# A fused attention and mixer kernel: the transposed copy of u made by VectorE and DMA instead of TensorE, and the second pass reordered

## The chip, the cores and the metric

The kernel runs on one core of one Trainium2 chip. The metric is the device time of one launch in microseconds (us). Before the change it is 831.86 us, the median of three runs from 831.58 to 831.9.

A core has five engines that run side by side, each with its own queue that it works through in order: TensorE (PE; its weight loads are listed as PEld), VectorE (DVE), ScalarE (ACT), GpSimd (POOL) and SyncE (SP). They wait for each other by semaphores. SP and ScalarE also issue DMAs, which sixteen DMA engines carry out.

## What is computed

```python
kv  = einsum('bhsd,bhse->bhde', k, v)            # 8 batches, 8 heads, 576 rows, 64 per head
out = einsum('bhsd,bhde->bhse', q, kv)
x   = out / sqrt(mean(out*out, -1) + 1e-6) * g   # then laid out as (8, 576, 512)
h   = maximum(x.T @ w_tok1, 0) @ w_tok2          # over the 576 rows, 256 in between
u   = x + h.T
out = u + maximum(u @ w_ch1, 0) @ w_ch2          # 512 -> 1536 -> 512
```

All is float32. The change concerns the last line, the "second pass" over u.

## The kernel before

**First pass.** Attention and token mixing run over pairs of batches and store u to DRAM (`u_dram`). Nine groups of 512 rows come of it: eight batches' first 512 rows, and one of the 64 remaining rows of each.

**Second pass.** For each group two products follow: u with w_ch1 (with relu), and the result v with w_ch2. Each is made by Strassen's scheme at two levels, so 7 x 7 = 49 block products in place of 64. A block product is three matmuls of 128 x 128 x 128. The blocks that go into them are sums of blocks: of u (`outer_u`, `inner_u`), of the weights (kept in DRAM as `sums_dram` and loaded 576 KB at a time into one of three `sums` tiles by `fetch_sums`), and of v (`split`, `inner`, the halves A, S1 to S4). Group 0 goes through `channel1_once` and `channel2_once` with one level only, while the weights' sums are made. Groups 1 to 8 go through `channel1(g, n0)` and `channel2(g, n0)`.

**Order.** The order of groups 1 to 8 is written by hand. A product has a place; the seven inner products of one outer product stand at the places of `PLACE`, and the next outer product begins seven places later, so that two are interleaved. `put(place, step)` sets steps of other engines behind a product. 49 places are a first product, the next 49 a second one, 98 a group. `keep` holds each engine to the order in which its instructions are written.

**Banks.** `outer` uses three PSUM banks. Bank a collects products 1, 6, 7 and 4, and is read after each of them (`read`: a copy on ScalarE, or an add on VectorE where `base` gives something to add). Bank c holds product 2, bank b products 5 and 3. `write` adds what was read to bank b or c, on VectorE. So product 6 must wait for the read after product 1, 7 for that after 6, 4 for that after 7, and product 3 for the `write` that reads bank b after product 5. Each has about two products' time for it.

**The transposed u.** The products need u with its columns on the partitions. `fetch_t` loads a tile of 128 rows x 512 from `u_dram` (`xt`, two buffers); `turn_u` transposes its four 128 x 128 blocks on TensorE into PSUM (`ps_ut`, line 515) and copies them to `uT` on ScalarE. For group g + 1 this happens in the second product of group g, at places 11, 15, 19 and 23 of it. There is one `uT`: it can be overwritten when the first product of group g is over. Its sums are made by VectorE at the end of the second product and at the start of the next group.

**Queues.** All of the second pass's DMAs are issued by SP: loads of the weights' sums (14 a group), of tiles of u (`xt` four, `xg` two, for the final sum) and stores of the result (two). Results of the second product are gathered in `r` tiles and added by VectorE (`radd`, `xadd`) to `xg`.

Of the kernel before, what the change touches and what calls it, by code (L numbers as in the profile page):

```python
# [19 lines left out]
def kernel(  # L20
# [85 lines left out]
    def do(f, *a):  # L106
        return lambda: f(*a)
# [394 lines left out]
    def fetch_t(g, i):  # L502

        if g < NG:
            xt[g, i] = late["xt"].tile([P, DM], F32, name="xt")
            dma(xt[g, i], u_dram[g][ts(i, P)])

    def turn_u(g, i, psum):
        if g >= NG:
            return  # L510
        if i == 0:
            uT[g] = late["u"].tile([P, 7, 7, P], F32, name="uT")
        pt = psum()
        for c in range(NC):
            keep(nc.tensor.transpose(pt[:, c], xt[g, i][:, ts(c, P)], ident))  # L515
        o, n = 2 * (i // 2), 2 * (i % 2)
        copy(uT[g][:, o:o + 2, n:n + 2], pt.rearrange("p (o n) t -> p o n t", o=2))

    def outer_u(g):

        return t_sums(lambda n: uT[g][:, SB[n], :4]) if g < NG else []

    def inner_u(g, lo, hi):

        return t_sums(lambda n: uT[g][:, lo:hi, SB[n]]) if g < NG else []

    V = {}

    def m_psum(shape, name):
        return late["m"].tile(shape, F32, name=name, tag="m")  # L530

    def t_psum():
        return late["t"].tile([P, NC, P], F32, name="ps_ut")

# [19 lines left out]
    def channel1_once(g):  # L554
# [4 lines left out]
        def pair(d):  # L559
# [3 lines left out]
            def product(n, ps, start, stop):  # L563
                for w in range(2):
                    i, f = divmod(2 * d + w, W)
                    for c in range(2):
                        wt = w_ch1[:, SA[n]] if SA[n] < 4 else late["w2"][:, SA[n] - 4]
                        matmul(ps[:, w], lhsT=wt[:, 2 * i + c, ts(f, P)],
                               rhs=uT[g][:, SB[n], c:4:2],
                               start=(start and w == 0 and c == 0), stop=stop,  # L570
                               skip_group_check=True)
# [104 lines left out]
    def outer(place, size, mul, to, base=None):  # L676
# [11 lines left out]
        def temp(n, bufs):  # L688
            t[n] = late["tmp"].tile([P, FQ], F32, name=n, tag=n, bufs=bufs)[:, :size]
            return t[n]  # L690

        def fit(flat, like):
            return flat if len(like.shape) == 2 else flat.rearrange("p (w t) -> p w t", w=W)

        def read(o, i, j):

            a = fit(banks["a"], to(i, j))
            o = fit(o, to(i, j)) if len(o.shape) == 2 else o
            if base:
                tensor_add(o, a, base(i, j))  # L700
            else:
                copy(o, a)

        def write(i, j, name, n):
            o = to(i, j)
            tensor_add(o, fit(banks[name], o), fit(t[n], o))

# [28 lines left out]

    ORDER1, ORDER2 = (1, 6, 2, 7, 5, 3, 4), (1, 4, 6, 5, 7, 2, 3)
    order = [(w, g, o) for g in range(1, NG) for w, os in ((1, ORDER1), (2, ORDER2)) for o in os]
    sums, v_in_parts = {}, {}

    def fetch_sums(n):
        if n < len(order):
            w, _, o = order[n]
            sums[n] = sums_tile()
            dma(sums[n], sums_dram[w, o])

# [5 lines left out]
    def channel1(g, n0):  # L752
# [4 lines left out]
        def first(i, o):  # L757
            n = n0 + i

            def mul(p, ps, start, stop):  # L760
                for w in range(W):
                    matmul(ps[:, ts(w, P)], lhsT=part(1, o, p, sums[n])[:, ts(w, P)],
                           rhs=uT[g][:, SB[o], SB[p]], start=(start and w == 0), stop=stop,
                           skip_group_check=True)

            base = {2: 1, 5: 3, 4: 1}.get(o)
            outer(7 * n, FQ, mul, lambda i, j: sub(v_tile(g, TO[o]), i, j),
                  base and (lambda i, j: sub(v_tile(g, base), i, j)))
            put(7 * n + PLACE[3] + 1, do(fetch_sums, n + 3))
# [15 lines left out]
        for t, *places in ((2, 25, 29, 28, 25), (7, 47, 47, 48, 48), (1, 53, 57, 53, 54)):  # L785
            for place, (i, j) in zip(places, ((0, 0), (0, 1), (1, 0), (1, 1))):
                rectify(place, t, i, j)
        if g > 1:
            steps = outer_u(g)[1:]
            for place, step in zip((0, 0, 2, 3, 4, 5, 7, 9), steps + [inner_u(g, 1, 2)[2]] + inner_u(g, 2, 7)):  # L790
                put(b + place, step)

    def channel2(g, n0):
# [3 lines left out]
        def second(i, o):  # L797
# [14 lines left out]

            outer(7 * n, P, mul, to)
            put(7 * n + PLACE[3] + 1, do(fetch_sums, n + 3))
            return r

        rs = {o: second(i, o) for i, o in enumerate(ORDER2)}

        def inner(o):
# [23 lines left out]

            return begin, steps[1], own if o == 1 else steps[2], steps[3]

# [28 lines left out]
        for place, steps in (  # L874
                (-17, [ins[1][0], ins[1][2]]), (-16, [ins[1][1]]), (-14, [ins[1][3]]),
                (1, [A[0], ins[4][0]]), (2, [A[1]]), (4, [ins[4][1], S1[0]]), (6, [ins[4][3], S1[1]]),
                (7, [ins[4][2]]), (8, [S2[0]]), (9, [S2[1]]), (11, [ins[6][0]]), (12, [S4[0]]),
                (13, [ins[6][1], S4[1]]), (15, [ins[6][3], ins[6][2]]), (17, [ins[5][0], S3[0]]),
                (19, [ins[5][1], S3[1]]), (20, [xadd(0, 0, 1)]), (21, [ins[5][3], ins[5][2]]),
                (23, [ins[7][0], xadd(1, 0, 4)]), (25, [ins[7][1]]), (26, [ins[7][2], ins[7][3]]),  # L880
                (28, [ins[2][0]]), (29, [radd(6, 1)]), (30, [ins[2][1], xadd(0, 1, 6)]),
                (32, [ins[2][3], ins[2][2]]), (34, [ins[3][0]]), (36, [xadd(0, 1, 5), ins[3][1]]),
                (37, [xadd(1, 1, 5)]), (38, [ins[3][3], ins[3][2]]), (43, [radd(7, 6)]),
                (44, [xadd(1, 0, 7)]), (45, [xadd(1, 1, 7)])):
            put(b + place, *steps)

        if g < NG - 1:
            for place, steps in ((57, [do(store, g, xg, 1)]), (59, [xadd(0, 0, 2)]), (63, [xadd(0, 1, 3)]),
                                 (71, [do(store, g, xg, 0)]), (78, [do(fetch_x, g + 1, 0)]),
                                 (85, [do(fetch_x, g + 1, 1)])):  # L890
                put(b + place, *steps)
        else:
# [4 lines left out]

            put(b + 49, xadd(0, 0, 2), do(store, g, xg, 1))
            put(b + 50, do(last, 0, 0))
# [3 lines left out]

        for i in range(J):
            place = b + 12 + 4 * i
            put(place - 12, do(fetch_t, g + 1, i)) if i < 2 else None
            put(place - 1, do(turn_u, g + 1, i, t_psum))
            put(place, do(fetch_t, g + 1, i + 2)) if i < 2 else None

        if g + 1 < NG:  # L910
            first, second, _, fourth = inner_u(g + 1, 0, 2)
            put(b + 40, first)
            put(b + 41, second)
            put(b + 42, fourth)
            put(b + 46, outer_u(g + 1)[0])
# [127 lines left out]
    late["xg"] = pool("xg", 1)  # L1043
    late["xt"] = pool("xt", 2)
    late["u"] = pool("u", 1)
    fetch_t(0, 0)
    fetch_t(0, 1)
    fill = [list(rounding), mix_ch1()]
    woven = fill[0][:4] + fill[1] + fill[0][4:]

    def turn(g, i, psum):
        turn_u(g, i, psum)
        if i + 2 < J:
            fetch_t(g, i + 2)

    u_psum = lambda: ps["o"].tile([P, NC, P], F32, name="ps_ut", tag="o")
    last = [
        "h00 2 -s40 2", "h01 2", "h10 2", "h11 2", "hr 1", "c0 u0 1", "c1 u1 1", "c2 u2", "c3 u3 1", "u4",
        "c4 u5 1", "u6 1", "u7", "u8"]
    more = {f"c{i}": do(turn, 0, i, u_psum) for i in range(J)}  # L1060
    more[f"c{J}"] = lambda: [f() for f in outer_u(0)]
# [3 lines left out]
    psums.close()  # L1065
    right.close()
    late["v"] = pool("v", 1, "right")
    late["r"] = pool("r", 4, "right")
# [4 lines left out]
    late["d2"] = pool("d2", 1, "right").tile([P, 3, NS, DH], F32, name="d2")  # L1073
    late["m"] = pool("m", 6, space=bass.MemoryType.PSUM)
    late["t"] = pool("t", 2, space=bass.MemoryType.PSUM)


    fetch_x(0, 0)
    fetch_x(0, 1)
    fetch_t(1, 0)  # L1080
    fetch_t(1, 1)
    firsts, lasts = mix_ch2()
    inner1 = [split(1, o) for o in ORDER1]
    inner2 = [split(2, o) for o in ORDER2]
    weave(channel1_once(0), firsts + [f for fs, _ in inner1 for f in fs])
    for n in range(3):
        fetch_sums(n)
    extra = [do(turn, 1, i, t_psum) for i in range(J)]
    extra += [lambda: [f() for f in outer_u(1)], lambda: [f() for f in inner_u(1, 0, 7)], lambda: None]
    body = [step for pair in zip(channel2_once(0), extra) for step in pair]  # L1090
    weave(body, lasts + [f for fs, _ in inner2 for f in fs] + [f for _, f in inner1])
# [49 lines left out]
```

## Time and profile before

| what | value |
|---|---|
| median of three runs | 831.86 us |
| the profiled execution | 832.03 us |
| its span, first to last instruction | 830.2 us |
| TensorE's transposes of u | 144, in 36 tiles, 188.8 to 738.9 us |
| ScalarE's copies of them | 36, 586 ns each |
| loads of sums, SP, 576 KB | 112, 3.8 us to landing |
| loads of u tiles, SP, 256 KB | 36, 3.5 us to landing |
| VectorE add, 128 / 384 / 512 / 768 elements | 283 / 548 / 680 / 948 ns |
| granted clock of TensorE | 0.999 |

The span is cut by stage: attention and token mixing to 206 us; group 0's first product to 243 and its second to 281; then eight groups of about 68 us to 826. Slices of the second pass look alike, so one group can be read for all:

```profile
416.60:484.90 68.30, 68.25 (x611) 68.02 (x610) 58.94 (x120) 22.78 (x61) 7.29 (x4) 1.00 0.53 172
484.90:553.20 68.30, 68.25 (x611) 68.02 (x610) 58.94 (x120) 22.90 (x61) 7.30 (x4) 1.00 0.53 169
```

The columns are the stretch in us, its length, busy time (and instructions) of PE, PEld, DVE, ACT and POOL, the granted clock, the share of the DMA engines and GB/s. A full engine is no proof that it sets the pace at every place: one also has to see in which half of a group each is full, and what waits for what there.

### The profile page before, as it was taken

The numbers are of one execution on the slowest core, as the hardware profiler recorded it, in microseconds if no ns is written. First come the engines' busy times: TensorE is split into PE (matmuls) and PEld (weight loads), VectorE is DVE, ScalarE is ACT, GpSimd is POOL, SyncE is SP. The second block draws the span as 40 slices with busy tenths as digits, with TensorE's granted clock in tenths as the row PEclk, the third lists the DMA queues.
The fourth block names the chain that finished last, engine by engine and source line by source line (L and its number), as shares of the span: only waits on it lengthen the run. The fifth ranks groups of instructions, "written<-read, shape, count | busy, mean of one in ns | idle before, by whom it ended". The sixth has DMA issues, their size and how long they took to land.

```text
span 830.2 us, 16562 instructions
## 1 busy us (share of the span) xinstructions
PE 812.6 (98%) x6528; PEld 719.9 (87%) x6528; DVE 701.8 (85%) x1334; ACT 289.1 (35%) x777; POOL 76.9 (9%) x59
## 2 busy tenths in 40 slices
PE   6999999999999999999999999999999999999997
PEld 6655555644888899999999999999999999999997
DVE  4688989999785979978977987997897897798696
ACT  1346665562210124234234323322423322333321
POOL 1200101010000020003003003001100300300300
PEclk9999999999999999999999999999999999999999
DMA  9999996422436445365356446546536545644642
GB/s 296 325 341 319 337 364 244 153 89 102 174 127 220 175 169 170 118 194 200 128 165 216 144 141 204 181 140 193 192 115 191 185 149 145 216 164 141 190 144 80
DMA packets 67966, 156.57 MB, mean 189 GB/s; under 512 B 5296, under 2 KB 24752, under 8 KB 67888
## 3 DMA queue, kind: packets, MB, share of 16 engines
q1 hardware_dynamic: 66208, 153.77, 56.6%
q10 hardware_dynamic: 1680, 1.74, 0.7%
q8 instruction: 52, 0.85, 0.4%
q14 instruction: 26, 0.21, 0.1%
HBM read 128.35 MB, written 27.13 MB: 187 GB/s over the span
## 4 chain that ended last, share of the span: by engine, by line
PE 88%; DVE 9%; issue 1%; DMA 1%; ACT 1%; SPq 0%; ACTq 0%; DVEq 0%
PE ps_a L127 35%; PE ps_b L127 18%; PE ps_c L127 9%; PE ps_h L127 6%; PE ps_u L127 6%; PE ps_v L127 4%; PE ps_w L127 3%; PE ps_o L127 3%; PE ps_ut L515 2%; PE ps_kv L127 2%; DVE sv L118 1%; DMA raw<-in_moe_w_tok_dram 1%; DVE v L118 1%; DVE x L379 1%; DVE ms L399 1%
## 5 line engine op out<-in xcount | busy, mean ns | idle before, releaser
L124 ACT COPY u<-ps_a 128x128 f32<-128x128 f32 (+1 forms) x176 | 60.5, 344 | 176.5 <-PE ps_a L127 164.6
L118 POOL TENSOR_TENSOR v<-v,v 128x768 f32<-128x768 f32 x32 | 58.4, 1856 | 553.0 <-ACT t L124 553.0
L127 PE MATMUL ps_b<-uT,sums 128*128 128x128 f32 x672 | 85.5, 275 | 0.0
L127 PEld LDWEIGHTS ps_b<-uT,sums 128*128 128x128 f32 x672 | 80.2, 192 | 0.0
L127 PE MATMUL ps_a<-uT,w_ch 128*128 128x128 f32 x576 | 78.8, 275 | 0.0
L127 PEld LDWEIGHTS ps_a<-uT,w_ch 128*128 128x128 f32 x576 | 71.5, 192 | 0.1
L118 DVE TENSOR_TENSOR v<-ps_b,u 128x384 f32<-128x384 f32 x112 | 60.2, 550 | 12.9 <-PE ps_b L127 12.9
L127 PE MATMUL ps_u<-h,w_tok 128*128 128x512 f32 (+1 forms) x160 | 67.0, 601 | 0.0
L127 PE MATMUL ps_h<-x,w_tok 128*128 128x512 f32 (+1 forms) x160 | 65.8, 603 | 0.8 <-ACT x L424 0.8
L118 DVE TENSOR_TENSOR v<-v,v 128x768 f32<-128x768 f32 (+1 forms) x70 | 64.1, 926 | 0.3
L118 DVE TENSOR_TENSOR uT<-uT 128x512 f32<-128x512 f32 (+4 forms) x103 | 63.1, 628 | 1.1
L124 ACT COPY t<-ps_a 128x128 f32<-128x128 f32 (+1 forms) x88 | 30.3, 344 | 92.7 <-PE ps_a L127 85.3
L121 ACT ACTIVATE v<-v 128x384 f32<-128x384 f32 (+1 forms) x102 | 49.3, 526 | 30.7 <-DVE v L118 26.6
L127 PE MATMUL ps_a<-uT,w 128*128 128x128 f32 x432 | 58.7, 275 | 0.0
L118 DVE TENSOR_TENSOR u<-ps_a,v 128x384 f32<-128x384 f32 x48 | 26.8, 558 | 32.1 <-PE ps_a L127 31.6
L127 PEld LDWEIGHTS ps_h<-x,w_tok 128*128 128x128 f32 (+1 forms) x160 | 25.9, 189 | 31.9 <-issue 28.1
L127 PEld LDWEIGHTS ps_a<-uT,w 128*128 128x128 f32 x432 | 53.4, 192 | 0.0
L118 DVE TENSOR_TENSOR xg<-xg,r 128x512 f32<-128x512 f32 (+1 forms) x78 | 50.7, 661 | 0.8 <-ACT r L124 0.6
L424 ACT ACTIVATE x<-x,inv 128x64 f32<-128x64 f32 x184 | 46.0, 335 | 9.5 <-DVE inv L419 8.1
L127 PE MATMUL ps_a<-uT,sums 128*128 128x128 f32 x336 | 46.9, 276 | 1.3 <-ACT t L124 1.3
L127 PE MATMUL ps_a<-sums,sv 128*128 128x128 f32 x336 | 47.3, 277 | 0.9 <-ACT r L124 0.5
L127 PEld LDWEIGHTS ps_u<-h,w_tok 128*128 128x128 f32 (+1 forms) x160 | 24.5, 179 | 27.1 <-issue 22.4
(123 smaller groups left out, 1650.1 us busy)
## 6 DMA issues: line engine op xcount, KB each, us to landing
sums<-sums SPq DMA_DIRECT2D x112, 576.0 KB, 3.8
qT<-in_q_dram SPq DMA_DIRECT2D x8, 1152.0 KB, 9.5
xt<-u_dram SPq DMA_DIRECT2D x36, 256.0 KB, 3.5
xg<-u_dram SPq DMA_DIRECT2D x18, 512.0 KB, 4.9
k_in<-in_k_dram SPq DMA_DIRECT2D x16, 512.0 KB, 9.2
u_dram<-x SPq DMA_DIRECT2D x16, 512.0 KB, 3.6
out_dram<-xg SPq DMA_DIRECT2D x16, 512.0 KB, 5.4
sums<-sv SPq DMA_DIRECT2D x14, 576.0 KB, 2.8
```

The costliest lines, as they stand in the source:

```text
L118: keep(engine.tensor_tensor(out=o, in0=a, in1=b, op=op))
L121: keep(nc.scalar.activation(o, a, AF.Relu))
L124: keep(nc.scalar.copy(o, a))
L127: keep(nc.tensor.matmul(*a, **kw))
L379: keep(nc.vector.tensor_mul(heads(X[pair, c][:, t]), heads(bank[c, t]), g_sb.to_broadcast([P, H, D])))
L399: keep(nc.vector.tensor_reduce(stats_of(c)[0][:, ts(t, H)], sq[c, t], axis=AX.X, op=ALU.add))
L424: keep(nc.scalar.activation(x[:, i], x[:, i], AF.Copy, scale=inv[:, i]))
L515: keep(nc.tensor.transpose(pt[:, c], xt[g, i][:, ts(c, P)], ident))
```

## The change

It has four parts, all in the second pass.

1. `turn_u` gives way to `turn_blocks` and `fetch_u`. VectorE transposes each 32 x 32 block of a tile within its 32 partitions (two instructions of 128 x 256 a tile) into `y`. After two tiles, four DMAs write `y` to DRAM (`blocks_dram`), and later four DMAs read it back so that the blocks come to lie as in the full transpose. `uT` gets the shape [128, 7, 4, 7, 32], so the sums and TensorE's moving operand read rows of 32. In groups 1 to 8 there is one buffer of `xt` and one of `y`; the turning stands in the first product (places 2 to 34), the reading back at places 8 and 10 of the second.
2. Sums are loaded on ScalarE's queue.
3. The outer products of the second product run in the order 1, 4, 2, 6, 5, 7, 3 in place of 1, 4, 6, 5, 7, 2, 3; product 6's read adds result 1 at once (so four VectorE reads in place of four ScalarE copies and one `radd`), and the steps beside the products get new places, some behind the product.
4. The two PSUM banks of the transposes go to the products (eight in place of six).

```diff
-            xt[g, i] = late["xt"].tile([P, DM], F32, name="xt")
+            xt[g, i] = late["xt" if g else "xt0"].tile([P, DM], F32, name="xt")
...
-        pt = psum()
-        for c in range(NC):
-            keep(nc.tensor.transpose(pt[:, c], xt[g, i][:, ts(c, P)], ident))
-        o, n = 2 * (i // 2), 2 * (i % 2)
-        copy(uT[g][:, o:o + 2, n:n + 2], pt.rearrange("p (o n) t -> p o n t", o=2))
+    def turn_blocks(g, i):
+        if g >= NG:
+            return
+        half, n = i // 2, 2 * (i % 2)
+        if n == 0:
+            xt[g] = late["y" if g else "y0"].tile([P, NC, 2, NC, Q], F32, name="y")
+        for o in range(2):
+            keep(nc.vector.transpose(
+                xt[g][:, :, o, n:n + 2].rearrange("p b n t -> p n b t"),
+                xt[g, i][:, ts(o, DH)].rearrange("p (n b t) -> p n b t", n=2, b=NC)))
+        if n:
+            t = blocks_dram[g, half] = dram.tile([Q, NC, 2, NC, P], F32, name=f"blocks{g}{half}")
+            for a in range(NC):
+                dma(t[:, :, :, a], xt[g][ds(a * Q, Q)].rearrange("p b o n t -> p b o (n t)"))
+
+    def fetch_u(g, half):
+        if g >= NG:
+            return
+        if half == 0:
+            uT[g] = late["u"].tile([P, 7, NC, 7, Q], F32, name="uT")
+        for b in range(NC):
+            dma(uT[g][ds(b * Q, Q), 2 * half:2 * half + 2, :, :4].rearrange("p o a n t -> p o a (n t)"),
+                blocks_dram[g, half][:, b])
...
-        return t_sums(lambda n: uT[g][:, lo:hi, SB[n]]) if g < NG else []
+        return t_sums(lambda n: uT[g][:, lo:hi, :, SB[n]]) if g < NG else []
...
-    ORDER1, ORDER2 = (1, 6, 2, 7, 5, 3, 4), (1, 4, 6, 5, 7, 2, 3)
+    ORDER1, ORDER2 = (1, 6, 2, 7, 5, 3, 4), (1, 4, 2, 6, 5, 7, 3)
...
-            dma(sums[n], sums_dram[w, o])
+            dma(sums[n], sums_dram[w, o], nc.scalar)
...
-                           rhs=uT[g][:, SB[o], SB[p]], start=(start and w == 0), stop=stop,
+                           rhs=uT[g][:, SB[o], :, SB[p]], start=(start and w == 0), stop=stop,
...
+        for place, f, i in ((2, fetch_t, 0), (16, turn_blocks, 0), (18, fetch_t, 1), (22, turn_blocks, 1),
+                            (24, fetch_t, 2), (28, turn_blocks, 2), (30, fetch_t, 3), (34, turn_blocks, 3)):
+            put(b + place, do(f, g + 1, i))
...
-            outer(7 * n, P, mul, to)
+            outer(7 * n, P, mul, to, o == 6 and (lambda i, j: rs[1][0][:, i, ts(j, P)]))
...
-            for place, steps in ((57, [do(store, g, xg, 1)]), (59, [xadd(0, 0, 2)]), (63, [xadd(0, 1, 3)]),
-                                 (71, [do(store, g, xg, 0)]), (78, [do(fetch_x, g + 1, 0)]),
+            for place, steps in ((58, [radd(7, 6)]), (60, [xadd(1, 1, 5)]), (61, [xadd(1, 0, 7)]),
+                                 (62, [xadd(1, 1, 7)]), (63, [do(store, g, xg, 1)]), (65, [xadd(0, 1, 5)]),
+                                 (66, [xadd(0, 1, 3)]), (71, [do(store, g, xg, 0)]), (78, [do(fetch_x, g + 1, 0)]),
...
-        for i in range(J):
-            place = b + 12 + 4 * i
-            put(place - 12, do(fetch_t, g + 1, i)) if i < 2 else None
-            put(place - 1, do(turn_u, g + 1, i, t_psum))
-            put(place, do(fetch_t, g + 1, i + 2)) if i < 2 else None
+        put(b + 8, do(fetch_u, g + 1, 0))
+        put(b + 10, do(fetch_u, g + 1, 1))
...
-    late["xt"] = pool("xt", 2)
+    late["xt"] = pool("xt", 1)
...
-    late["m"] = pool("m", 6, space=bass.MemoryType.PSUM)
-    late["t"] = pool("t", 2, space=bass.MemoryType.PSUM)
+    late["y"] = pool("y", 1, "right")
+    late["m"] = pool("m", 8, space=bass.MemoryType.PSUM)
```

For groups 0 and 1 the turning is woven into the end of the first pass and into group 0's first product, with two buffers each for group 0.

## The prediction

> **What bounds the kernel now.** I read the page's busy totals and chain of waits first, then the timeline of TensorE over one group of the second pass, then VectorE's over the same group, and last the stretches of that group in a table of windows.
>
> ```profile
> PE 812.6 (98%) x6528; PEld 719.9 (87%) x6528; DVE 701.8 (85%) x1334; ACT 289.1 (35%) x777; POOL 76.9 (9%) x59
> ...
> PE 88%; DVE 9%; issue 1%; DMA 1%; ACT 1%; SPq 0%; ACTq 0%; DVEq 0%
> ```
>
> TensorE is never without work; 88% of the chain that ends last is TensorE. In the second pass (from 280.7 us) the timeline of TensorE shows, in start, duration and group:
>
> ```profile
> 349.06 0.83 PE L127 MATMUL ps_a<-uT,w_ch 128*128 128x128 f32 x6
> 349.73 0.83 PE L127 MATMUL ps_c<-uT,w_ch 128*128 128x128 f32 x6
> ...
> 389.93 0.60 PE L515 MATMUL ps_ut<-ident,xt 128*128 128x128 f32 x4
> 390.36 0.93 PE L127 MATMUL ps_b<-w_ch,sv 128*128 128x128 f32 x6
> ...
> 416.85 0.83 PE L127 MATMUL ps_a<-uT,w_ch 128*128 128x128 f32 x6
> ```
>
> A block product (three matmuls) starts 0.67 us after the one before; four transposes of u take 0.43. A group, from one first product to the next, takes 416.85 - 349.06 = 67.79: 98 products are 65.66, sixteen transposes 1.74, and 0.4 is waits. The windows of this group (length, then PE, PEld, DVE, ACT, POOL busy, clock, DMA share, GB/s) are its first product, most of its second, and the rest:
>
> ```profile
> 349.06:382.56 33.50, 33.50 (x303) 33.50 (x302) 24.79 (x47) 11.64 (x26) 7.29 (x4) 1.00 0.57 176
> 382.56:411.08 28.52, 28.47 (x255) 28.23 (x254) 28.48 (x60) 9.99 (x30) 0.00 (x0) 1.00 0.49 165
> 411.08:416.85 5.77, 5.77 (x55) 5.77 (x53) 5.15 (x14) 1.07 (x4) 0.00 (x0) 1.00 0.46 157
> ```
>
> The second line is the one to see: during the second product VectorE is busy 28.48 of 28.52 us. Two engines are full there, and the transposes that TensorE does in that stretch are also time in which VectorE catches up. In the first product VectorE has 8.7 us to spare, ScalarE much everywhere.
>
> [...]
>
> **The change part by part.**
>
> Transposes off TensorE. 36 tiles by four: 36 x 0.435 = 15.7 us of the chain gone: 4 tiles at 188.8 to 195.8 and 4 at 247.9 to 265.2 (together 3.5), and 28 in the seven groups that prepare a next one (1.74 each). ScalarE's 36 copies (587 ns) go too, off the path.
>
> Transposes on VectorE: 72 of 128 x 256. [...] I take 0.44, and as VectorE's rows overlap by 0.08 (384-element rows last 0.55 and start 0.47 apart), 0.365 spacing, 0.81 for a tile's pair from start to end. Low end 0.35; high end 0.69[...]. Per group 8 x 0.365 = 2.9 us, all in the first product, where 8.7 are free. By total it fits: VectorE's work in a group, each instruction at its spacing, goes from 56.7 to 59.7, below 65.7. The question is order.
>
> The order on VectorE in the first product (built program, times from the group's start, product n starting at 0.67n). One buffer each holds the loaded tile and its turned blocks. Tile 0's pair stands behind product 15 and ends at 11.7. Only then can SP load tile 1. Landing of these loads in this group of before, in us:
>
> ```profile
> DMA to landing us min/median/max: 2.6/3.4/4.2
> ```
>
> At 3.4 tile 1 is there at 15.2; VectorE comes to it at 14.5, waits, ends at 16.0. Now SP issues four writes of the turned blocks (0.43 each, as its stores of xg took) before the load of tile 2: 16.0 + 1.7 = 17.7, landing at 21.1. Meanwhile VectorE has two adds of 768 (0.87) and four of 384 (0.47), 3.6 us, and is at tile 2 at 19.6: it stands for 1.5 us. Queued behind it are the write-out that frees bank b for product 31, and the read u2 that product 32 waits for. 21.1 + 0.81 + 0.55 = 22.4 against 31 x 0.67 = 20.8: TensorE waits 1.6, then 0.3 more for u2. Sum 1.9; with landings of 2.6 it is 0.4, with 4.2 it is 3.6; with transposes of 0.69 add 1.0. Tile 3 is covered: its load goes out at 21.9, and eight adds (3.8) stand before its pair.
>
> The second product without its transposes. From the read behind product 46 to the read t1 behind product 70 VectorE now has 17 instructions of 384 elements, 8 of 768, 8 of 128 with t1, and one of 512: 8.0 + 7.0 + 1.6 + 0.6 = 17.2, and 0.2 for start and end. TensorE has 24 products, 16.1. Product 71 waits for t1: 1.3 late. Products 70 to 76 carry 5.6 us of VectorE work against 4.7: another 0.3. So 1.6; I bound it by 1.0 and 2.0. Before, 17.75 us of such work stood against 16.1 + 1.74 + waits, and just fitted: that cover goes with the transposes. The new order moves radd and xadd work behind the product, but sixth's reads (four of 128) become VectorE's, and the pair of adds for 2 comes forward.
>
> Sums on ScalarE's queue: 14 issues a group. ACT's DMA issues took a median of 0.57 on the store of the rest, so 8 us on an engine 22.7 busy of 67.8. Each stands behind the copy u3 of the outer product that follows; the next copy has 1.34 - 0.48 us before TensorE needs it. Hidden: zero. It waits on no recent DMA: in the program each one's semaphore was last used many products earlier. If a wait did fall there, copies and TensorE would stand behind it.
>
> More DMA: 16 transfers of 128 KB a group in rows of 512 B, 4096 packets. The page's third part gives 0.7% of 16 engines for 1680 packets of about 1 KB, 55 ns each; at 55 at most 4096 / 16 x 55 = 14 us of 68, DMA share 0.53 to under 0.75. The reads of the blocks start at products 57 and 59, with 30 products before the first sum of uT: hidden. Sums and matmuls now read runs of 32: VectorE's rows over 64-element heads (682 ns for 512) cost what flat ones do (680), so zero; for TensorE no row shows it: between zero and 5% of the first product, 1.6 us a group; I take zero.
>
> Sum: a preparing group is 65.66 + 0.2 of old waits + 1.9 + 1.6 = 69.36, 1.57 more than 67.79. Seven of them: +11.0; first stages -3.5, as VectorE (37.56 of 40.00 busy from 166 to 206) gets four tiles there with the turned u not needed before 206. The profiled execution took 832.03 (span 830.2 and 1.8 around), so 839.5; it stood 0.2 above the median of 831.86, so 839.3.
>
> **The rivals.** (a) Likeliest, slower by the two stalls: 0.58; own range 831 to 848. (b) Faster: VectorE absorbs it. The mechanism is its 8.7 free us in the first product: if loads land in 2.6 and VectorE is ahead at product 46, TensorE loses 0.4 and about 0.5; group 66.8, 832.0 - 3.5 - 7 x 1.0 = 821.5. It decides when both stalls together fall below 67.79 + 3.5 / 7 - 65.66 - 0.2 = 2.4 a group. For it: the free time, landings of 2.6 when nothing runs beside. Against: a sums load and a 512 KB store run beside tile 1's load, and the 17.2 of the second product. 0.15. (c) VectorE's transposes cost 0.69 or TensorE reads short runs slower: 1.0 to 2.0 more a group, 847 to 853; for it only that no row shows either. 0.20. (d) Gain and stalls cancel, within 1.7 us (0.2%, what a measurement of this kernel can tell from no change): landings of 2.9, which make the first stall 1.0. 0.07. That it does not do what it says is excluded by the built program, which has no transposes on TensorE.
>
> **How the numbers follow.** 839.3 is (a). The range 826 to 853 leaves out the best of (b) and the tail of (c). Faster 0.15, same 0.07, slower 0.78.
>
> **What would show it.** Right: no ps_ut rows; transposes near 0.44 us; VectorE idle before the third tile's pair, ended by a DMA; TensorE waits on DVE v (bank b) and r or t in every group; group pitch 69.4. Wrong: pitch below 67.8, or TensorE waits on ScalarE or on uT's landing, or products not 0.67 apart.

## The result, and the profile after

The changed kernel takes 875.51 us (median of 4 runs, 874.69 to 877.14) against 831.88 for the kernel before (now the median of four): a ratio of 1.0528, 95% interval 1.0509 to 1.0546. The profiled execution took 877.14 us, its span is 875.4. The forecast was 839.3 us. The direction was right, the size was not: 43.6 us were lost, not 7.4.

The page's busy totals and its chain of waits, for the changed kernel:

```profile
PE 819.2 (94%) x6384; PEld 720.7 (82%) x6384; DVE 733.9 (84%) x1430; ACT 258.9 (30%) x709; POOL 78.3 (9%) x59
...
PE 59%; DVE 24%; DMA 10%; issue 3%; SPq 2%; ACT 1%; ACTq 0%; DVEq 0%
```

TensorE's share of the chain fell from 88% to 59%. VectorE rose from 9% to 24%, transfers from 1% to 10%. TensorE has 144 instructions fewer and yet is busy for longer (819.2 against 812.6 us): some of its matmuls ran slower. Both, the waits and the slower matmuls, show in one group. The trace records each matmul of a block product twice, so x6 is one product and x12 two. Products are counted here from 426.07, two after the group's first one, because the last two of the group before stand in between; tiles are counted from 0. The timeline of the changed kernel, all engines, in the first product of the group that starts at 426.07 (start, duration, engine, operation, and in brackets the idle time before it and what ended that):

```profile
440.82 0.77 DVE L521 STREAM_TRANSPOSE y<-xt 128x256 f32<-128x256 f32 x2
441.62 2.52 SPq L115 DMA_DIRECT2D blocks<-y  x4
443.99 0.33 ACTq L115 DMA_DIRECT2D sums<-sums  x1
444.19 0.95 SPq L115 DMA_DIRECT2D xt<-u_dram  x1
446.39 0.83 PE L127 MATMUL ps_b<-uT,sums 128*128 128x128 f32 x6
449.88 0.77 DVE L521 STREAM_TRANSPOSE y<-xt 128x256 f32<-128x256 f32 x2 [4.71 <-DMA xt<-u_dram]
450.57 0.52 DVE L118 TENSOR_TENSOR v<-ps_b,u 128x384 f32<-128x384 f32 x1
451.14 1.65 PE L127 MATMUL ps_b<-uT,sums 128*128 128x128 f32 x6 [3.92 <-DVE v L118]
452.59 2.77 PE L127 MATMUL ps_a<-uT,w 128*128 128x128 f32 x12
```

Read it from the top: VectorE turns tile 1; SP issues the four writes of the turned blocks until 444.14; ScalarE's queue starts a load of sums at 443.99; SP's load of tile 2 goes out at 444.19. VectorE comes to tile 2 at 445.17, stands for 4.71 us, turns it, and only then (450.57) empties the bank that product 31 needs. TensorE has waited 3.92 us. And the products that follow run at half speed: 2.77 us for twelve recorded matmuls that take 1.50 elsewhere (at 436.79, for one). The windows of the same group (length, then PE, PEld, DVE, ACT, POOL busy, clock, DMA share, GB/s) are its products 0 to 30, the wait, what follows it, and the rest:

```profile
426.07:446.80 20.73, 20.73 (x186) 20.59 (x185) 18.11 (x34) 7.22 (x17) 0.00 (x0) 1.00 0.71 215
446.80:451.14 4.34, 0.42 (x4) 0.23 (x3) 1.26 (x4) 0.00 (x0) 0.00 (x0) 0.83 0.68 258
451.14:456.47 5.33, 5.33 (x25) 5.33 (x26) 4.64 (x10) 0.48 (x1) 1.17 (x1) 0.50 0.55 161
456.47:500.41 43.94, 42.96 (x379) 42.42 (x379) 38.29 (x83) 11.50 (x35) 6.35 (x4) 1.00 0.59 163
```

The clock column is 1.00, then 0.50 behind the wait, then 1.00 again. In the kernel before it was 1.00 throughout such a group.

From the starts of all matmuls in the trace, less 0.67 us for each product, I work out where each of the seven preparing groups loses time (mean, us a group). What the half clock costs is in the third row, with whatever else is lost there:

| part of the group | before | after | forecast |
|---|---|---|---|
| products 0 to 29 | 0.27 | 0.64 | 0.2 |
| wait ahead of product 31 | 0 | 4.32 | 1.6 |
| products 31 to 38 | 0 | 2.39 | 0.3 |
| products 58 to 97 (before: with 1.74 of transposes) | 2.13 | 1.73 | 1.6 |
| whole group (98 products are 65.66) | 68.06 | 74.76 | 69.36 |

Seven groups: 7 x (74.76 - 68.06) = 46.9. The second pass starts 3.5 earlier (277.19 against 280.73), the last group takes 74.9 instead of 73.05: 46.9 - 3.5 + 1.8 = 45.2, the difference of the spans.

### The profile page after: what moved, and what is told of

It reads as the page before. It is cut to its first block, busy times and chain, and to the rows that moved or that the text cites. A ratio compares the mean times of both kernels' runs of the same rounds, so it can differ in the third digit from the quotient of the medians.

```text
span 875.4 us, 16466 instructions
## 1 busy us (share of the span) xinstructions
PE 819.2 (94%) x6384; PEld 720.7 (82%) x6384; DVE 733.9 (84%) x1430; ACT 258.9 (30%) x709; POOL 78.3 (9%) x59
## 4 chain that ended last, share of the span: by engine, by line
PE 59%; DVE 24%; DMA 10%; issue 3%; SPq 2%; ACT 1%; ACTq 0%; DVEq 0%
PE ps_a L127 22%; PE ps_b L127 12%; DMA xt<-u_dram 6%; DVE v L118 6%; PE ps_c L127 5%; PE ps_u L127 5%; PE ps_v L127 4%; PE ps_h L127 4%; DVE sv L118 4%; DMA uT<-blocks 2%; SPq L115 2%; PE ps_o L127 2%; PE ps_w L127 2%; DVE y L521 2%; PE ps_kv L127 2%
## 5 line engine op out<-in xcount | busy, mean ns | idle before, releaser
L127 PE MATMUL ps_b<-uT,sums 128*128 128x128 f32 x672 | 91.6, 284 | 29.3 <-DVE v L118 29.3
L124 ACT COPY u<-ps_a 128x128 f32<-128x128 f32 (+1 forms) x160 | 56.1, 351 | 193.1 <-PE ps_a L127 162.7
L127 PEld LDWEIGHTS ps_b<-uT,sums 128*128 128x128 f32 x672 | 84.0, 198 | 31.0 <-DVE v L118 30.8
L124 ACT COPY t<-ps_a 128x128 f32<-128x128 f32 (+1 forms) x80 | 28.1, 351 | 175.2 <-PE ps_a L127 157.5
L127 PE MATMUL ps_a<-uT,w 128*128 128x128 f32 x432 | 68.0, 305 | 0.0
L127 PEld LDWEIGHTS ps_a<-uT,w 128*128 128x128 f32 x432 | 62.8, 221 | 0.2 <-DVE u L118 0.2
L521 DVE STREAM_TRANSPOSE y<-xt 128x256 f32<-128x256 f32 x72 | 27.6, 421 | 38.4 <-DMA xt<-u_dram 33.4
```

Of the source, the lines that this page charges most:

```text
L124: keep(nc.scalar.copy(o, a))
L127: keep(nc.tensor.matmul(*a, **kw))
L521: keep(nc.vector.transpose(xt[g][:, :, o, n:n + 2].rearrange("p b n t -> p n b t"), xt[g, i][:, ts(o, DH)].rearrange("p (n b t) -> p n b t ...
```

## The experiments

Theories beforehand. 1: the load of tile 2 goes out late, behind four writes, and a single buffer passes this on to TensorE. Rival A: the load is slow because of what runs beside it. Rival B: the sums on ScalarE's queue. Rival C: the new order of the second product. 2: the half clock is a consequence of the wait. 3: the waits in the second product are VectorE's backlog.

**The load ahead of the writes.** The four writes are issued behind the load of tile 2.

```diff
-        if n:
+        if n and (i == 3 or g < 2):
+            write_blocks(g, half)
...
-                            (24, fetch_t, 2), (28, turn_blocks, 2), (30, fetch_t, 3), (34, turn_blocks, 3)):
+                            (24, fetch_t, 2), (24, write_blocks, 0), (28, turn_blocks, 2), (30, fetch_t, 3),
+                            (34, turn_blocks, 3)):
```

> The changed kernel, with the four writes of the first two turned tiles put behind the load of tile 2 on SP's queue instead of ahead of it; nothing else. Theory 1 (the load of tile 2 goes out late because it stands behind four writes of 0.60 us each, and one buffer makes VectorE, the bank's reader and TensorE wait for it): it goes out 2.5 us earlier, VectorE stands about 2 instead of 4.7 us, TensorE waits about 1.5 instead of 4.2 at product 31, its clock does not fall to 0.5, and a group lasts 68 to 69 us: 830 to 840 us in all. Rival A (the load lands late because its packets share the DMA engines with the writes, the store and a load of sums, wherever it stands in the queue): it lands as late as before, group above 73, 865 or more. Rival B (the sums on ScalarE's queue) and rival C (the new order): no change, 875.

Measured: 879.14 us, ratio to before 1.0579 (1.0546 to 1.0612). A miss. What VectorE waits for, in the changed kernel and then in this one (us in total, times, longest):

```profile
DVE y L521 <- DMA xt<-u_dram: 33.4, 10, 5.5
```

```profile
DVE y L521 <- DMA blocks<-y: 32.7, 7, 5.2
```

In the same group the load of tile 2 now went out 2.6 us earlier (0.03 us behind the transposes) and landed in 4.4, so that it would have cost VectorE 0.8 us of standing in place of 4.7. But the turning of tile 2 writes into the same `y` that the four writes still read; these, now later, took 3.9 to 6.4 us to land, VectorE stood for 4.98, and the wait took their name. VectorE waits for two transfers that share one queue; swapping them swaps which ends last. The changed kernel shows it already: there the last write lands only 0.6 us before the load in this group (449.18 and 449.80), so the load alone had little to gain. Theory 1 is right about single buffers, wrong in that the place in the queue alone would cure it.

**The turnings later.** Only places are moved.

```diff
-                            (24, fetch_t, 2), (28, turn_blocks, 2), (30, fetch_t, 3), (34, turn_blocks, 3)):
+                            (24, fetch_t, 2), (36, turn_blocks, 2), (38, fetch_t, 3), (46, turn_blocks, 3)):
```

> The changed kernel with only the places of the last turnings moved: tile 2 turned at product 36 instead of 28, the load of tile 3 at 38 instead of 30, tile 3 turned at 46 instead of 34. Theory 1: the load of tile 2 goes out and lands as late as before, but VectorE comes to it 5.4 us later, finds it there, and the wait of 4.2 us at product 31 and the half clock behind it are gone; what is left is 1.0 us of waits in the second product, and up to 1 us where VectorE comes late into it: group 66.7 to 68.0, 822 to 832 us. Rival A agrees here with theory 1. Rivals B and C: the wait stays where it is or only moves, 865 or more.

Measured: 831.94 us, ratio to before 1.0003 (0.9994 to 1.0012). The wait ahead of product 31 and the half clock are gone in all groups (0.0 in both rows of the table); the window of one group:

```profile
414.76:482.38 67.62, 66.64 (x591) 65.96 (x589) 61.12 (x129) 19.24 (x53) 7.31 (x4) 1.00 0.67 201
```

So this one wait with what follows it cost all that was lost. It is not DMA traffic as such: the same transfers are made, at a higher mean share (0.67, against 0.63 in the changed kernel's groups).

**Sums on SP's queue again.**

```diff
-            dma(sums[n], sums_dram[w, o], nc.scalar)
+            dma(sums[n], sums_dram[w, o])
```

> The changed kernel with the weight sums loaded on SP's queue again, as in the kernel before. Theory 1: the load of tile 2 is still behind the four writes, so the wait at product 31 and the half clock stay: 870 to 880 us. Rival B (the loads of sums on ScalarE's queue [...]run beside tile 2's load): the wait falls to about 2 us, group near 69, 840 to 850 us.

Measured: 856.75 us, ratio 1.0307 (1.0276 to 1.0339): between the two forecasts and 18.8 us less than the changed kernel, so rival B has a part, though not all. The landing of tile 2's load in one group, in the changed kernel and then here:

```profile
DMA to landing us min/median/max: 5.6/5.6/5.6
```

```profile
DMA to landing us min/median/max: 2.9/2.9/2.9
```

Over the seven groups it is 5.0 to 6.4 in the changed kernel and 2.8 to 5.1 here. On SP's queue the load of sums that ran ahead of tile 2's load is issued 0.6 us behind it. From the first write's issue to tile 2's landing it is now 6.4 us instead of 8.2 in this group; the wait falls from 4.32 to 2.16 (mean of the seven).

**One load of sums later.** To tell the queue from the neighbour, one load a group is put three products later, on ScalarE's queue as the others.

```diff
-            put(7 * n + PLACE[3] + 1, do(fetch_sums, n + 3))
+            put(7 * n + PLACE[3] + (4 if i == 2 else 1), do(fetch_sums, n + 3))
```

> The changed kernel with one load of sums a group put later on ScalarE's queue: the one that stands at product 27, just ahead of the load of tile 2, goes to product 30. All sums stay on ScalarE's queue. If what the sums cost (19 us when all go back to SP) is this one load running beside the load of tile 2, tile 2 lands in 3 to 4 instead of 5.6 us, TensorE waits about 2 to 3 us, and the total is 850 to 865 us. If it is the queue of ScalarE in general: 873 to 880 us.

Measured: 860.56 us, ratio 1.0344 (1.0327 to 1.0362). Tile 2 lands in 3.7 in the same group (2.9 to 4.2 over the seven), the wait is 2.09. Four fifths of what moving all sums back saved comes from this one load. It is rival A in the form of one neighbour: 576 KB that start 0.2 us ahead of the 256 KB that VectorE stands for (0.2 to 1.6 us ahead in six groups, just behind in the first).

**Sums on ScalarE's queue, alone.** The kernel before, with this edit only:

```diff
-            dma(sums[n], sums_dram[w, o])
+            dma(sums[n], sums_dram[w, o], nc.scalar)
```

> The kernel before with the second part of the change alone: the sums loaded on ScalarE's queue. If the 19 us that the sums cost the changed kernel come only from their running beside the load of tile 2 that VectorE waits for, nothing waits closely for a load here and it costs nothing: 830.5 to 833.5 us. Rival (loads on ScalarE's queue hold up its copies[...], in any kernel): 836 us or more.

Measured: 832.42 us, ratio 1.0006 (0.9998 to 1.0015). The same edit that costs the changed kernel 18.8 us costs nothing that can be told where no engine stands for a load beside it.

**Waits of measured length.** The kernel before, with useless additions on VectorE ahead of the bank of product 31.

```diff
+    idle = pool("idle", 1, "right").tile([P, 4 * P], F32, name="idle")
+    keep(nc.vector.memset(idle, 0.0))
+    def load_vector(g):
+        for _ in range(g + 2):
+            tensor_add(idle, idle, idle)
...
+        put(b + 28, lambda: load_vector(g))
```

> The kernel before, with additions of 128 x 512 on VectorE that nobody reads, put ahead of the bank that product 31 needs: three in group 1, one more in each later group, ten in group 8, 0.60 us each. It measures what a wait of TensorE costs beyond its own length. Theory 2 (TensorE's clock falls to half after an idle stretch[...])[...]. Rival (the half clock in the changed kernel has another cause, such as the DMA traffic or the reads in runs of 32): the clock stays at 1.0 in all groups and each is longer by its wait alone, 1.4 to 5 us; in all some 860 us.

Measured: 872.25 us (one run; what counts is its groups against each other). TensorE's timeline in the second group and in the third:

```profile
373.06 0.94 PE L127 MATMUL ps_b<-uT,sums 128*128 128x128 f32 x6 [1.21 <-DVE v L118]
373.98 1.60 PE L127 MATMUL ps_a<-uT,w 128*128 128x128 f32 x12
```

```profile
443.31 0.94 PE L127 MATMUL ps_b<-uT,sums 128*128 128x128 f32 x6 [1.94 <-DVE v L118]
444.24 2.93 PE L127 MATMUL ps_a<-uT,w 128*128 128x128 f32 x12
```

A wait of 1.21 us leaves the next twelve matmuls at 1.60; one of 1.94 makes them 2.93. The clock over these stretches, with a third one from a group with a wait of 4.12:

```profile
371.00:376.00 5.00, 3.79 (x32) 3.42 (x31) 4.93 (x11) 0.35 (x2) 0.00 (x0) 1.00 0.51 152
441.00:447.00 6.00, 4.06 (x23) 3.69 (x22) 5.59 (x12) 0.00 (x0) 0.00 (x0) 0.76 0.48 158
661.00:669.60 8.60, 5.96 (x28) 5.96 (x29) 6.80 (x13) 0.48 (x1) 1.81 (x1) 0.60 0.38 130
```

| group | 1 | 2 | 3 | 4 | 5 | 6 | 7 |
|---|---|---|---|---|---|---|---|
| wait ahead of product 31, us | 0.49 | 1.21 | 1.94 | 2.67 | 3.39 | 4.12 | 4.85 |
| lost in products 31 to 38, us | 0.36 | 0.36 | 1.92 | 1.69 | 2.67 | 2.84 | 2.58 |
| recorded matmuls of product 31 (six), us | 0.94 | 0.94 | 0.94 | 1.65 | 1.65 | 1.65 | 1.65 |
| the twelve behind them, us | 1.60 | 1.60 | 2.93 | 2.43 | 2.77 | 2.77 | 2.77 |

Theory 2 holds: no turned u, no short runs and fewer transfers are in this kernel, and waits alone bring the half clock. In this run those of 1.94 us and more did, those of 0.49 and 1.21 did not. Beyond the 0.36 that a short wait leaves behind, the half clock costs 1.3 to 2.5 us in this kernel.

**The new order alone.** The kernel before, with the new order of the second product and the new places of the steps beside it (of the edit, the order and product 6's read are shown); TensorE still transposes.

```diff
-    ORDER1, ORDER2 = (1, 6, 2, 7, 5, 3, 4), (1, 4, 6, 5, 7, 2, 3)
+    ORDER1, ORDER2 = (1, 6, 2, 7, 5, 3, 4), (1, 4, 2, 6, 5, 7, 3)
...
-            outer(7 * n, P, mul, to)
+            outer(7 * n, P, mul, to, o == 6 and (lambda i, j: rs[1][0][:, i, ts(j, P)]))
```

> The kernel before with the third part of the change alone: the new order of the second product's block products, its places of additions and the read of product 6 on VectorE. TensorE still transposes u, and SP still loads the sums. Theory 3 (the waits of 1.66 us a group in the second product of the changed kernel come from VectorE, which has 17.2 us of work beside 16.1 us of products and no transposes to catch up in): with the transposes back the order costs nothing, group 67.3 to 67.9, 829 to 833 us. Rival C (the new order itself makes products 59, 71 and 77 wait): the waits of 1.66 are there beside the 1.74 of transposes, group 69.0 to 69.6, 840 to 846 us.

Measured: 831.25 us, ratio 0.9996 (0.9987 to 1.0004), group 67.50. Rival C falls: the order brings no wait while the transposes are there.

**Three additions on GpSimd.** From here on all are changed kernels with the later places of tiles 2 and 3 (831.94).

```diff
-        xadd = lambda i, j, o: do(lambda: tensor_add(quarter(i, j), quarter(i, j), rs[o][0]))
+        xadd = lambda i, j, o: do(lambda: tensor_add(quarter(i, j), quarter(i, j), rs[o][0],
+                                                     engine=nc.gpsimd if o in (1, 2, 4) else nc.vector))
```

> The changed kernel with the later places of tiles 2 and 3 (as in the run before, 831.9 us), and the three additions of 128 x 512 for block products 1, 4 and 2 into x done by GpSimd, not VectorE. Theory 3 (VectorE's load): 3 x 0.6 = 1.8 us less on VectorE between products 46 and 80 a group, so the waits of 1.66 us at products 59, 71 and 77 fall below 0.6; group 66.4 to 66.9, 820 to 826 us. Rival (these waits are the latency of one read after one product, whatever else VectorE does): they stay, 831 to 833 us. Rival (GpSimd is too slow for the tiles r to come free, or slows VectorE): above 834 us.

Measured: 833.45 us, ratio 1.0020 (1.0012 to 1.0028). The timeline in one group, GpSimd's line and VectorE's beside it:

```profile
458.57 0.55 DVE L118 TENSOR_TENSOR sv<-v,sv 128x384 f32<-128x384 f32 x1
458.87 2.32 POOL L118 TENSOR_TENSOR xg<-xg,r 128x512 f32<-128x512 f32 x1 [12.40 <-DVE r L118]
...
460.37 1.24 DVE L118 TENSOR_TENSOR sv<-sv,v 128x384 f32<-128x384 f32 x1
```

VectorE's last addition of 384 here takes 1.24 us, begun beside GpSimd's; the 56 of its kind (`sv<-sv,v`) in the kernel before have a mean of 0.548. VectorE is no freer than before (728.9 us busy, 725.2 without the edit), so this run says nothing on theory 3.

**The same, with the sums on SP's queue.**

> As the run with additions on GpSimd, and the sums on SP's queue again. If the waits of 0.8 to 1.0 us at product 29 in two of the groups come from a load of u that runs beside a load of sums, they go, and 1 to 4 us are gained: 818 to 824 us. If SP's queue is too full with both: 826 us or more.

Measured: 832.38 us, ratio 1.0007 (0.9998 to 1.0015). The waits at product 29 (in groups 2 and 5) went, but waits of 0.1 to 0.6 us at products 36 and 57, most of them for a load of sums, stand in four groups (0.18 at product 36 in two groups before). The forecast of 818 to 824 us missed. Inconclusive: the waits at product 29 are worth some 0.3 us a group, and what ends them I did not settle.

**Three additions left out.** x lacks the terms of block products 1, 4 and 2.

```diff
-                (12, [S2[1]]), (13, [ins[2][3], ins[2][2]]), (14, [ins[6][0]]), (15, [xadd(0, 0, 1)]),
+                (12, [S2[1]]), (13, [ins[2][3], ins[2][2]]), (14, [ins[6][0]]),
...
-                (22, [ins[5][0]]), (23, [xadd(1, 0, 4)]), (24, [ins[5][1]]), (25, [ins[5][3], ins[5][2]]),
+                (22, [ins[5][0]]), (24, [ins[5][1]]), (25, [ins[5][3], ins[5][2]]),
```

(and the one for 2 at place 32)

> The changed kernel with the later places of tiles 2 and 3, and the additions of block products 1, 4 and 2 into x left out (three of 128 x 512 on VectorE a group), so x lacks these terms. GpSimd does nothing in their place. Theory 3: 1.8 us less on VectorE, of which 0.6 before the read that product 71 needs: the waits of 1.66 us fall below 1.1, group 66.4 to 67.0, 820 to 827 us. With this no lower than the run that moved two of them, the third matters nothing. Rival (latency): 831 to 833 us.

Measured: 825.62 us, ratio 0.9930 (0.9914 to 0.9945). The loss from product 58 on falls from 1.75 to 0.97 us a group: with less work on VectorE there is less waiting, as theory 3 has it.

**Two additions later.** Nothing is left out.

```diff
-(15, [xadd(0, 0, 1)])
+(25, [xadd(0, 0, 1)])
...
-(23, [xadd(1, 0, 4)])
+(31, [xadd(1, 0, 4)])
```

> The changed kernel with the later places of tiles 2 and 3, and two of VectorE's additions into x moved behind the wait at product 71: the one for block product 1 from place 15 to 25 of the second product, the one for 4 from 23 to 31. No work is taken away. Theory 3 (the waits at products 59 to 77 are VectorE's backlog, 17.2 us of work against 16.1 before the read that product 71 needs): one addition less before that read, so the wait at 71 falls from 0.97 to about 0.4 us and the group from 67.6 to about 67.0: 826 to 829 us. Rival (the waits are a latency that does not depend on VectorE's backlog): 831 to 833 us.

Measured: 828.69 us, ratio 0.9963 (0.9948 to 0.9977); 1.28 us from product 58 on. The start of product 71 is 0.27 late instead of 0.87: 0.6 less, the time from one addition of 512 to the next on VectorE, and one was moved past it. Theory 3 holds for the waits from product 71 on: they are backlog. The wait ahead of product 59 did not change.

**More of it moved.** Besides, the second half of a21 three products earlier, and other steps by one or two products.

```diff
-                (1, [A[0], ins[4][0]]), (2, [A[1]]), (3, [ins[4][1]]), (4, [S1[0]]), (5, [ins[4][3]]),
+                (-1, [A[1]]), (1, [A[0], ins[4][0]]), (3, [ins[4][1]]), (6, [S1[0]]), (6, [ins[4][3]]),
...
+                (29, [xadd(0, 0, 1)]), (31, [ins[7][1]]), (31, [xadd(0, 0, 2)]), (31, [ins[7][3], ins[7][2]]),
+                (34, [ins[3][0]]), (35, [xadd(1, 0, 4)]), (37, [ins[3][1]]), (38, [xadd(0, 1, 6)]),
```

> As the run before it, with a further piece of VectorE's work moved out of the crowded stretch: the second half of the addition that makes a21 three products earlier, to the end of the first product, and small moves of one or two products for others. Theory 3: the group falls to 66.2 to 66.8 us, 818 to 825 us, and the kernel is faster than both. Rival: 830 to 833 us.

Measured: 822.06 us, ratio to before 0.9884 (0.9869 to 0.9898): faster than both. The window of one group and the chain of waits:

```profile
412.97:479.39 66.42, 66.15 (x590) 65.82 (x589) 60.96 (x129) 19.20 (x53) 7.30 (x4) 1.00 0.69 205
```

```profile
PE 71%; DVE 21%; issue 3%; DMA 2%; ACT 1%; ACTq 0%; SPq 0%; DVEq 0%
```

The waits from product 71 on are gone (but for 0.4 us in one group); the 0.53 us around product 59 are left, as in nearly all groups of all runs that turn u on VectorE. TensorE waits there for an addition on VectorE; why that one comes late no run shows. This group is 1.37 us shorter than in the kernel before: most of the 1.74 that the transposes took on TensorE, once neither a load nor VectorE's backlog takes it back.

## Why the prediction was wrong in size

1. **Transposes off TensorE, -3.5 us in the first stages**: right. The second pass starts 3.5 us earlier.
2. **A transpose on VectorE at 0.44 us, 0.81 for a pair**: right. No row of before shows the 0.44, as none is a transpose on VectorE; its additions of 128 and 384 elements (283 and 548 ns) give 0.42 for 256 by interpolation. The row of the tile in one group (ns, minimum, median, maximum) and pairs of 0.77:

```profile
L521 DVE STREAM_TRANSPOSE y<-xt x8: 402/419/445, 437.0 to 455.4; 128x256 f32<-128x256 f32 x8
```

3. **The wait ahead of product 31, "Sum 1.9"**: the place, the mechanism and the form of the sum were right; this is the step that failed. The forecast was 1.7 for the writes and 3.4 for the landing, less the 3.6 that VectorE has to do meanwhile: 1.5 of standing. The trace has 2.57 (0.64 from one issue to the next, not 0.43, which came from stores of another shape) and 5.61, less 3.55: 4.7 of standing. The landing of 3.4 was the middle of four loads in a group of before, of which the trace shows two that went out just ahead of a load of sums (2.6) and two just behind one (4.1 and 4.2). Tile 2's load has a load of sums ahead of it and the last writes beside it. The forecast looked at what runs beside tile 1's load and not at tile 2's; for this one 4.2 was the figure to start from, not the far end. Nor did it have the landing of the four writes, for which VectorE waits too. With the one load of sums moved, VectorE still stands for 2.8 us. Against the 1.9, products 30 to 38 lost 4.32 + 2.39 = 6.71.
4. **Not in the sum at all: the half clock.** The prediction priced a wait of up to 3.6 us as its own length and 0.3 more. A wait up to 1.21 us does leave 0.36 behind in the kernel before; the changed kernel loses 2.39 there, at a clock of 0.50 from 451.14 to 456.47 in the group shown. That a wait brings this, the added waits show. But not all of the 2.39 is the clock's. With the sums on SP's queue three groups kept the full clock and lost 1.53 there all the same: 0.36, and 1.17 at product 38, where TensorE waits for VectorE again. One of these groups:

```profile
593.90 3.90 POOL L118 TENSOR_TENSOR v<-v,v 128x768 f32<-128x768 f32 x2 [62.99 <-DVE v L118]
594.33 1.79 DVE L118 TENSOR_TENSOR sv<-v,sv 128x384 f32<-128x384 f32 x1
596.65 0.94 PE L127 MATMUL ps_b<-uT,sums 128*128 128x128 f32 x6 [0.91 <-DVE v L118]
```

VectorE's addition takes 1.79 us beside GpSimd's, not 0.55. Three groups of that run with a half clock behind the wait lost 1.97 to 1.99, only 0.45 more: while TensorE is slow, VectorE catches up (no wait stands at product 38 in these three; in the other three it is 0.91 us). From these groups I estimate the clock's own share in the changed kernel at 2.39 - 1.53, some 0.9 us a group; no run takes it apart there.
5. **The second product, "another 0.3. So 1.6"**: the sum was right, in part by luck. 1.73 were measured, as 0.53 around product 59, 0.97 around 71 and 0.24 around 77; the forecast had it all at 71 and after, where it is 1.21. That backlog is the cause of these 1.21 was shown by moving the additions; the 0.53 did not move with them.
6. **"Sums on ScalarE's queue ... Hidden: zero"**: wrong in the changed kernel (18.8 us), right in the kernel before (no difference). I asked what is queued behind the issue on ScalarE, and priced issue time alone; that nothing else moves no trace of before showed, as all its sums are loaded on SP's queue. The trace of the changed kernel shows a load that no longer stands in SP's line run ahead of and beside what SP issues next: 576 KB, issued at 443.99, ahead of the 256 KB load issued at 444.19, which landed in 5.6 us, not 2.9. What it delayed was the one load that bounded the group.
7. **Short runs of 32 at zero**: right; a product of the first product starts 0.67 us after the one before, as it did.
8. **The end**: not considered. The last group is 1.8 us longer: in the trace two stores issued on ScalarE (1.46 us) now stand ahead of the copy that the last addition needs. No run tried this.

By size: 7 x (6.71 - 1.9) = 33.7 us of the miss of 37.6 in the profiled execution lie in step 3 and the clock behind it, about 19 in the wait and 15 in what follows it, of which some 6 are the clock's own by the estimate above. The rest is the end, the waits ahead of product 30 (less 1.9 us that the first group lost there already before), and the second product's extra 0.13.

## What to carry to other kernels

Where an engine in the chain stands for a load, price that load by what will run beside it after the change, not by its landing today, and ask of every transfer that changes queue what it now runs beside. Give a single-buffered tile its distance in time before you trust its place in a queue: eight products later cost nothing here and was worth 43 us. And do not price a wait of TensorE at its own length alone: here 4.32 us ahead of product 31 were followed by a half clock and 2.39 us more, of which some 0.9 were the clock's own by the estimate above.

## What was not expected of the hardware

The forecast had no half clock behind a wait. With added waits in the kernel before, 0.49 and 1.21 us were followed by twelve recorded matmuls in 1.60 us, 1.94 to 4.85 us by the same twelve in 2.43 to 2.93. The length alone doesn't decide. With the sums on SP's queue, waits of 1.74, 1.86 and 1.90 us had these twelve behind them in 2.93, 2.89 and 2.93 us, and waits of 1.62, 1.69 and 1.90 us in 1.60. Two groups of that run with the same wait:

```profile
302.54 0.97 PE L127 MATMUL ps_b<-uT,sums 128*128 128x128 f32 x6 [1.90 <-DVE v L118]
303.47 2.93 PE L127 MATMUL ps_a<-uT,w 128*128 128x128 f32 x12
```

```profile
661.74 0.94 PE L127 MATMUL ps_b<-uT,sums 128*128 128x128 f32 x6 [1.90 <-DVE v L118]
662.67 1.60 PE L127 MATMUL ps_a<-uT,w 128*128 128x128 f32 x12
```

So a wait of 1.90 us was followed by the half clock in one group and not in another; these lengths do not tell the two apart.
